# Moving the second half of each attention unit's transposes and products one slot earlier

## The chip, the cores and the metric

The kernel runs on one core of one Trainium2 chip. The metric is the device time in microseconds of one execution; three runs of the kernel before have a median of 1816.32 us.

## The reference

Linear attention over 8 batches, 8 heads, 576 tokens and a head width of 64, then two MLPs over the 4608 tokens:

```python
q_s = exp(q - max(q, -1)); q_s /= sum(q_s, -1) + 1e-9
k_s = exp(k - max(k, 2));  k_s /= sum(k_s, 2) + 1e-9
kv = einsum('bhsd,bhse->bhde', k_s, v)
x = einsum('bhsd,bhde->bhse', q_s, kv)            # to (4608, 512)
xn = x / sqrt(mean(x * x, -1) + 1e-6) * rms_g
y = (silu(xn @ w_gate) * (xn @ w_val)) @ w_out    # d_ff 1536
h = y @ w_in
out = (h * sigmoid(1.702 * h)) @ w2_out           # d_ff 2048
```

## The kernel before

All products are made of three passes over numbers split in a high and a low part (hi, lo). The first MLP runs over 9 tiles of 512 tokens (j = 0 to 8). A tile has 36 slots, three for each of its 12 chunks of the hidden width: slot 3n is the long product with w_gate (wg, 12 matmuls), slot 3n+1 the one with w_val (wv), slot 3n+2 the output product of the chunk before (into ps_acc, weights wo). The second MLP follows in a part of its own, which the change does not reach.

In the gaps between the long products of tile j stands the attention of batch j+1: four units (c = 0 to 3) of two heads each, for the tiles 0 to 6. The steps of a unit (unit_steps, from line 303 on) are:

- s0: maximum of k over the tokens of a partition (DVE, L316). s1: transpose of it (L323) and its maximum (L327); q less its maximum (L330, L331). s2: transpose back (L335) and k less the maximum (L336).
- s3: the exponentials of k and q (ACT, L354: ke, qe); loads of the next unit's k, q and v on SP; the sums of qe and their reciprocals (DVE, L360 to L362); qe divided by them (L363: on POOL for batches 0 and 1, so in tile 0, and on DVE from tile 1 on).
- s4: k times v, 20 small matmuls (L370); on DVE its normalisation into kvH and kvL, the high and low part (L378 to L385).
- qT(0), qT(1): transposes of the first and second half of qe (L399), copied to qH (ACT, L407) and qL (DVE, L408). The halves are 256 and 320 tokens wide; in even batches (odd tiles) the first half is the one of 256, two transposes, and in odd batches that of 320, a narrow transpose and two full ones.
- att(0), att(1): three matmuls with kvH and kvL for each half (L414 to L416), copied to xr (ACT, L422).

The order is written by hand. The table AT (L782) gives the slot of each of the nine steps, to which 6c is added for unit c; within a slot the long product and what belongs to it come first, then the steps in the order of units, then what else is put there. After the steps, `squares(c)` is put at the slot AT[-1] + 6c (L797): ACT squares the unit's xr (L439, L442), and for c > 0 DVE adds it (L444). Slots of the part 0 end with `split_out_weight` (from tile 1 on), which splits a weight into wo on ACT (L160) and POOL (L161). In tile 0 the weights are also decoded in every slot (L148 to L157). In slot 30 `total` sums the squares on PE (L449).

All PSUM banks of these steps come from one pool of two, in the order in which the steps are recorded:

```python
bufs = {"att": 2, "gv": 2, "acc": 4}[tag]
return ps.tile([P, 512], F32, tag=tag, bufs=bufs, name=f"ps_{tag}")
...
order = sorted((AT[s] + 6 * c, c, s) for c in range(len(mine)) for s in range(STEPS))
...
put(j, AT[-1] + 6 * c, squares, c)
```

Of the kernel before, what the change touches and what calls it, by code (L numbers as in the profile page):

```python
# [20 lines left out]
def attention_glu_mlp(  # L21
# [708 lines left out]
    with tc.manual_schedule():  # L730
# [48 lines left out]
        def put(j, slot, fn, *args):  # L779
            plan[j][slot].append(lambda: fn(*args))  # L780

        AT = (-1, 1, 2, 3, 4, 6, 7, 9, 10)  # L782

        for j in range(NTILE):
            mine = [(j + 1) * NC + c for c in range(NC) if (j + 1) * NC + c < len(units)]
            for c, u in enumerate(mine):
                steps[u] = unit_steps(u)
            order = sorted((AT[s] + 6 * c, c, s) for c in range(len(mine)) for s in range(STEPS))
            for slot, c, s in order:
# [4 lines left out]
            if j + 1 < NTILE:  # L794
                squares, total, spread, scale = norm_steps(j + 1)
                for c in range(NC):
                    put(j, AT[-1] + 6 * c, squares, c)  # L797
                put(j, 30, total)
# [275 lines left out]
```

## Time and profile before

| what | us |
|---|---|
| median of three runs (1816.26 to 1817.03) | 1816.32 |
| the profiled execution | 1816.74 |
| its span, first to last instruction | 1814.9 |
| PE busy, whole span | 1742.3 (96%) |
| DVE busy | 1203.9 (66%) |
| ACT busy | 779.9 (43%) |
| POOL busy | 396.1 (22%) |

The engines are PE (TensorE), DVE (VectorE), ACT (ScalarE), POOL (GpSimd) and SP, which here issues loads and stores. Times within the span are in microseconds from its start. Tile 0 lies from 59.1 to 212.6, tile 1 from 212.6 to 324.2, and so on by 111.6 us to tile 6; the last two tiles have no attention. A matmul's end in the profile is modelled, so rows of PE overlap a little.

### The profile page before, as it was taken

What the parts mean: (1) busy time and instruction counts of PE and PEld (TensorE: products, weight loads), DVE (VectorE), ACT (ScalarE), POOL (GpSimd) and SP (SyncE); (2) the same over time, 40 slices, a digit from 0 to 9 for tenths busy, and PEclk for the clock granted to TensorE, in tenths of its full rate; (3) what the DMA queues carried; (4) which work ended last, traced back from release to release, by engine and by line L of the source; (5) the groups of instructions that cost most, each with busy time, mean ns of one, the idle gap of its engine ahead of it and who ended that gap; (6) DMA issues with size and microseconds to landing.
All of it is one profiled execution on the core that took longest, in us unless ns stands there. A gap on an engine that the chain in (4) does not pass through costs nothing.

```text
span 1814.9 us, 26699 instructions
## 1 busy us (share of the span) xinstructions
PE 1742.3 (96%) x10092; PEld 1543.3 (85%) x10092; DVE 1203.9 (66%) x2017; ACT 779.9 (43%) x1304; POOL 396.1 (22%) x360
## 2 busy tenths in 40 slices
PE   5777999999999999999999999999999999999998
PEld 4565788888888888888888879999999899999998
DVE  7999875775757657575323347556546797777785
ACT  4555544444444444443312236444435543333332
POOL 4666512212121221211111434000002640000000
PEclk9898999999999999999999999999999999999999
DMA  5344341322323232220001015434444544444432
GB/s 156 124 134 127 101 123 55 106 84 67 103 65 105 75 95 75 60 75 20 24 1 47 24 58 186 140 113 141 140 148 159 197 129 139 129 128 128 128 117 82
DMA packets 202001, 186.31 MB, mean 103 GB/s; under 512 B 58256, under 2 KB 183696, under 8 KB 201872
## 3 DMA queue, kind: packets, MB, share of 16 engines
q1 hardware_dynamic: 191888, 166.51, 29.7%
q10 hardware_dynamic: 9984, 18.09, 2.7%
q8 instruction: 79, 1.29, 0.3%
q14 instruction: 50, 0.41, 0.1%
HBM read 119.54 MB, written 65.01 MB: 102 GB/s over the span
## 4 chain that ended last, share of the span: by engine, by line
PE 85%; DVE 10%; issue 2%; DMA 1%; ACT 1%; POOL 0%; SPq 0%; DVEq 0%; ACTq 0%; POOLq 0%
PE ps_gv L493 29%; PE ps_in L639 19%; PE ps_out L984 17%; PE ps_acc L493 15%; PE ps_att L370 1%; PE ps_att L399 1%; DVE uf L722 1%; DVE w L151 1%; DVE raw L151 1%; DVE raw L550 1%; DVE raw L154 1%; DVE u L509 1%; PE ps_att L449 1%; DVE y L998 0%; DVE m L316 0%
## 5 line engine op out<-in xcount | busy, mean ns | idle before, releaser
L984 PE MATMUL ps_out<-w2o,uf 128*128 128x256 f32 x3024 | 366.8, 284 | 5.4 <-DVE uf L722 4.7
L984 PEld LDWEIGHTS ps_out<-w2o,uf 128*128 128x128 f32 x3024 | 365.1, 193 | 7.1 <-DVE uf L722 5.6
L639 PE MATMUL ps_in<-xf,w2i 128*128 128x384 f32 x2016 | 349.9, 334 | 2.4 <-ACT ev L530 2.4
L639 PEld LDWEIGHTS ps_in<-xf,w2i 128*128 128x128 f32 x2016 | 349.4, 188 | 3.1 <-ACT ev L530 2.8
L493 PE MATMUL ps_acc<-u,wo 128*128 128x512 f32 x1296 | 328.6, 403 | 5.7 <-POOL wo L161 5.7
L493 PE MATMUL ps_gv<-xs,wg 128*128 128x512 f32 x1296 | 322.5, 397 | 7.1 <-POOL wg L161 5.6
L493 PE MATMUL ps_gv<-xs,wv 128*128 128x512 f32 x1296 | 319.2, 395 | 0.4 <-DVE s L834 0.4
L493 PEld LDWEIGHTS ps_gv<-xs,wg 128*128 128x128 f32 x1296 | 243.4, 191 | 62.4 <-POOL wg L161 7.7
L493 PEld LDWEIGHTS ps_acc<-u,wo 128*128 128x128 f32 x1296 | 244.9, 193 | 58.6 <-POOL wo L161 6.8
L493 PEld LDWEIGHTS ps_gv<-xs,wv 128*128 128x128 f32 x1296 | 240.6, 189 | 49.4 <-POOL wv L161 1.2
L161 POOL TENSOR_TENSOR wo<-raw,wo 128x512 fp32r<-128x512 f32 x108 | 142.3, 1318 | 495.5 <-ACT wo L160 477.5
L828 ACT ACTIVATE s<-ps_gv 128x512 f32<-128x512 f32 x108 | 64.5, 598 | 428.6 <-PE ps_gv L493 428.6
L834 DVE TENSOR_TENSOR s<-s,ps_gv 128x512 f32<-128x512 f32 x108 | 73.9, 684 | 198.3 <-PE ps_gv L493 174.3
L624 ACT ACTIVATE h<-h 128x384 f32<-128x384 f32 x144 | 74.4, 525 | 115.2 <-DVE h L661 85.1
L157 POOL TENSOR_TENSOR w<-w,stage 128x512 int32<-128x512 int32 x56 | 73.5, 1312 | 220.2 <-DVE w L154 70.9
L550 DVE TENSOR_TENSOR raw<-raw 128x256 f32<-128x256 f32 (+1 forms) x236 | 108.0, 500 | 11.8 <-DMA raw<-w2d 7.6
L661 DVE TENSOR_TENSOR h<-h,ps_in 128x384 f32<-128x384 f32 x144 | 78.0, 553 | 49.8 <-PE ps_in L639 49.3
L719 ACT ACTIVATE uf<-raw 128x1792 fp32r<-128x1792 f32 x36 | 61.2, 1701 | 86.0 <-PE ps_out L984 53.1
L554 POOL TENSOR_TENSOR w2o<-raw,w2o 128x256 fp32r<-128x256 f32 x35 | 28.2, 843 | 275.9 <-DMA u<-h 270.1
L722 DVE TENSOR_TENSOR uf<-raw,uf 128x1792 fp32r<-128x1792 f32 x36 | 74.4, 2067 | 18.7 <-ACT uf L719 18.7
L510 DVE TENSOR_TENSOR u<-s,u 128x512 fp32r<-128x512 f32 x108 | 82.8, 767 | 3.7
L360 DVE TENSOR_REDUCE qs<-qe 128x10 f32<-128x640 f32 x32 | 26.2, 820 | 85.7 <-ACT qe L354 85.6
(139 smaller groups left out, 1863.2 us busy)
## 6 DMA issues: line engine op xcount, KB each, us to landing
u<-h SPq DMA_DIRECT2D x192, 192.0 KB, 1.9
stage<-in_moe_w_out_dram SPq DMA_DIRECT2D x28, 512.0 KB, 3.6
raw<-u SPq DMA_DIRECT2D x24, 512.0 KB, 4.3
x<-ev ACTq DMA_DIRECT2D x36, 256.0 KB, 2.0
stage<-in_moe_w_in_dram SPq DMA_DIRECT2D x16, 512.0 KB, 3.7
w2d<-w SPq DMA_DIRECT2D x32, 256.0 KB, 3.3
v_sb<-in_v_dram SPq DMA_DIRECT2D x60, 128.0 KB, 3.2
out_dram<-y ACTq DMA_DIRECT2D x30, 256.0 KB, 4.3
```

Of the source, the lines that this page charges most:

```text
L157: return lambda: nc.gpsimd.tensor_tensor(dst, dst, lo, op=ALU.add)
L161: nc.gpsimd.tensor_tensor(dst[:, 1, :], src, f(dst[:, 0, :]), op=ALU.subtract)
L493: nc.tensor.matmul(t, w(a), x(e), start=first and i == 0, stop=last and i == 2)
L510: nc.vector.tensor_tensor(u[:, 1, :], s, f(u[:, 0, :]), op=ALU.subtract)
L550: engine.tensor_tensor(raw[:, o], raw[:, a], raw[:, b], op=op)
L624: nc.scalar.activation(dst, src, AF.Gelu_apprx_sigmoid)
L639: nc.tensor.matmul(t, w[:, a, s, c * P : (c + 1) * P], xfac[i, p, c][:, e, :], start=p in (1, 6, 5) and c == 0 and k == 0, stop=c == 1 and ...
L661: nc.vector.tensor_tensor(v, v, t, op=ALU.add)
L722: nc.vector.tensor_tensor(w[:, 1], raw, f(w[:, 0]), op=ALU.subtract)
L828: nc.scalar.activation(s, tg, AF.Silu)
L834: nc.vector.tensor_tensor(s, s, tv, op=ALU.mult)
L984: nc.tensor.matmul(t[:, i * Q : (i + 1) * Q], u[:, a, LEFT[p] - 1, i * P : (i + 1) * P], w[:, e, m % 2, :], start=m == 0 and i == 0 and n ...
```

## The change

Two entries of the table: the second transposes qT(1) go from slot 7 to slot 6, behind the first, and the second products att(1) from slot 10 to slot 9, behind the first. As `squares` takes its slot from the last entry, it moves a slot ahead as well.

```diff
-        AT = (-1, 1, 2, 3, 4, 6, 7, 9, 10)
+        AT = (-1, 1, 2, 3, 4, 6, 6, 9, 9)
```

On PE, around the transposes of the second unit of tile 1 (wg, wv are the long products, x12 is twelve matmuls in a row; the waits are on semaphores of the engine named), before:

```order
L493 MATMUL ps_gv<-xs,wg_977 128x512 x12
L399 MATMUL ps_att<-ident,qe 128x128 [waits DVE_49,PE_49,Activation_49]
L399 MATMUL ps_att<-ident,qe 128x128
L493 MATMUL ps_gv<-xs,wv_1033 128x512 [waits DVE_49]
L493 MATMUL ps_gv<-xs,wv_1033 128x512 x11
L399 MATMUL ps_att<-ident,qe 128x128 [waits DVE_49,PE_49]
L399 MATMUL ps_att<-ident,qe 128x128
L399 MATMUL ps_att<-ident,qe 128x64
L323 MATMUL ps_att<-ident,m_2212 128x128 [waits DVE_49]
```

and now:

```order
L493 MATMUL ps_gv<-xs,wg_986 128x512 x12
L399 MATMUL ps_att<-ident,qe 128x128 [waits DVE_49,PE_49,Activation_49]
L399 MATMUL ps_att<-ident,qe 128x128
L399 MATMUL ps_att<-ident,qe 128x128 [waits DVE_49,PE_49]
L399 MATMUL ps_att<-ident,qe 128x128
L399 MATMUL ps_att<-ident,qe 128x64
L493 MATMUL ps_gv<-xs,wv_1033 128x512 x12
L323 MATMUL ps_att<-ident,m_2212 128x128 [waits DVE_49]
```

The second half, with its wait on DVE, stands ahead of the wv product; s1 of the next unit stays behind it.

On ACT, from the copy of the second unit's first att half on, tile 1, before:

```order
L422 ACTIVATE xr<-ps_att 128x256
L354 ACT_TABLE_LOAD
L354 ACTIVATE ke<-k_sb 128x2x5x64
L354 ACTIVATE qe<-q_sb 128x2x5x64
L160 ACTIVATE wo<-raw_1088 128x512
L422 ACTIVATE xr<-ps_att 128x320
L442 ACTIVATE sqb<-xr 128x512
```

and now:

```order
L422 ACTIVATE xr<-ps_att 128x256
L422 ACTIVATE xr<-ps_att 128x320
L354 ACT_TABLE_LOAD
L354 ACTIVATE ke<-k_sb 128x2x5x64
L354 ACTIVATE qe<-q_sb 128x2x5x64
L442 ACTIVATE sqb<-xr 128x512
L160 ACTIVATE wo<-raw_1095 128x512
```

The second copy stands ahead of the next unit's exponentials, and the square ahead of the weight's copy.

On DVE, in the third unit of tile 1, from the division of qe to kvL, before:

```order
L363 TENSOR_TENSOR qe<-qe,qs 128x640
L834 TENSOR_TENSOR s<-s,ps_gv 128x512
L509 CAST u<-s 128x512
L510 TENSOR_TENSOR u<-s,u 128x512
L378 TENSOR_SCALAR rs<-ps_att 128x1
L379 RECIPROCAL rs<-rs 128x1
L382 TENSOR_SCALAR kvH_76<-ps_att,rs 64x64 x2
L385 SCALAR_TENSOR_TENSOR kvL_78<-ps_att,rs,kvH_76 64x64 x2
L444 TENSOR_TENSOR sqa<-sqa,sqb 128x512
```

and now:

```order
L363 TENSOR_TENSOR qe<-qe,qs 128x640
L444 TENSOR_TENSOR sqa<-sqa,sqb 128x512
L834 TENSOR_TENSOR s<-s,ps_gv 128x512
L509 CAST u<-s 128x512
L510 TENSOR_TENSOR u<-s,u 128x512
L378 TENSOR_SCALAR rs<-ps_att 128x1
L379 RECIPROCAL rs<-rs 128x1
L382 TENSOR_SCALAR kvH_76<-ps_att,rs 64x64 x2
L385 SCALAR_TENSOR_TENSOR kvL_78<-ps_att,rs,kvH_76 64x64 x2
```

The addition of the squares stands ahead of the steps that make kvL.

## Rows read from the trace of the kernel before

**Rows 1.** Windows, tiles 0 and 1: us; busy PE, PEld, DVE, ACT, POOL; clock, DMA, GB/s.

```profile
59.10:212.60 153.50, 121.82 (x540) 93.09 (x538) 148.48 (x194) 86.40 (x148) 97.93 (x72) 0.88 0.43 132
212.60:324.20 111.60, 111.58 (x577) 90.96 (x576) 73.98 (x135) 51.00 (x87) 24.45 (x19) 1.00 0.28 84
```

**Rows 2.** Timeline of DVE, tile 1: start, us, what, [idle before <- releaser].

```profile
246.20 0.82 DVE L360 TENSOR_REDUCE qs<-qe 128x10 f32<-128x640 f32 x1 [3.57 <-ACT qe L354]
247.05 1.03 DVE L361 TENSOR_SCALAR qs<-qs 128x10 f32<-128x10 f32 x1
248.36 0.83 DVE L363 TENSOR_TENSOR qe<-qe,qs 128x640 f32<-128x640 f32 x1
...
251.91 0.60 DVE L385 SCALAR_TENSOR_TENSOR kvL<-ps_att,rs,kvH 64x64 fp32r<-64x64 f32 x2
...
271.89 0.70 DVE L444 TENSOR_TENSOR sqa<-sqa,sqb 128x512 f32<-128x512 f32 x1
272.50 1.32 DVE L316 TENSOR_REDUCE m<-k_sb 128x128 f32<-128x640 f32 x1
```

**Rows 3.** Timeline of PE, tile 1, around the second unit's steps.

```profile
242.42 0.28 PE L414 MATMUL ps_att<-qH,kvH 128*128 128x256 f32 x1
...
246.02 0.95 PE L370 MATMUL ps_att<-v_sb,ke 128*64 128x65 f32 x20
...
252.48 0.38 PE L399 MATMUL ps_att<-ident,qe 128*128 128x128 f32 x2
...
255.45 0.58 PE L399 MATMUL ps_att<-ident,qe 128*128 128x128 f32 x3
```

**Rows 4.** Timelines: kvL and first transposes, tile 1 unit 0, tile 2 unit 1.

```profile
233.01 0.60 DVE L385 SCALAR_TENSOR_TENSOR kvL<-ps_att,rs,kvH 64x64 fp32r<-64x64 f32 x2
233.14 0.38 PE L399 MATMUL ps_att<-ident,qe 128*128 128x128 f32 x2
...
363.63 0.60 DVE L385 SCALAR_TENSOR_TENSOR kvL<-ps_att,rs,kvH 64x64 fp32r<-64x64 f32 x2
...
364.26 0.64 PE L399 MATMUL ps_att<-ident,qe 64*128 64x64 f32 x3
```

**Rows 5.** Timeline of ACT and POOL, tile 1, around the second unit's exponentials.

```profile
243.11 0.38 ACT L422 ACTIVATE xr<-ps_att 128x256 f32<-128x256 f32 x1
...
244.80 0.74 ACT L354 ACTIVATE ke<-k_sb 128x640 f32<-128x640 f32 x1
245.44 0.72 ACT L354 ACTIVATE qe<-q_sb 128x640 f32<-128x640 f32 x1
246.07 0.61 ACT L160 ACTIVATE wo<-raw 128x512 fp32r<-128x512 f32 x1
246.59 0.47 ACT L422 ACTIVATE xr<-ps_att 128x128 f32<-128x128 f32 x2
...
246.76 1.29 POOL L161 TENSOR_TENSOR wo<-raw,wo 128x512 fp32r<-128x512 f32 x1 [2.69 <-ACT wo L160]
246.96 0.63 ACT L439 ACTIVATE sqa<-xr 128x512 f32<-128x512 f32 x1
```

**Rows 6.** Timelines of POOL and DVE, tile 0: L361 free, L510 under POOL.

```profile
68.44 0.17 DVE L361 TENSOR_SCALAR qs<-qs 128x10 f32<-128x10 f32 x1
...
73.58 1.48 POOL L161 TENSOR_TENSOR wv<-w,wv 128x512 fp32r<-128x512 f32 x1
73.94 1.67 DVE L510 TENSOR_TENSOR u<-s,u 128x512 fp32r<-128x512 f32 x1
```

**Rows 7.** Waits of PE, whole span: us in total, times, longest us.

```profile
PE ps_att L449 <- DVE sqa L444: 4.0, 2, 2.0
```

**Rows 8.** Timelines of PE and DVE, tile 0.

```profile
92.33 0.31 PE L414 MATMUL ps_att<-qH,kvH 128*128 128x320 f32 x1
...
93.44 0.81 DVE L336 TENSOR_TENSOR k_sb<-k_sb,ps_att 128x640 f32<-128x640 f32 x1
...
101.98 2.56 PE L493 MATMUL ps_gv<-xs,wg 128*128 128x512 f32 x10 [1.63 <-POOL wg L161]
```

## The prediction

> **What bounds the kernel now.** I read the busy time by stretch first [rows 1]. In tile 0 (59.1 to 212.6 us) VectorE (DVE) is busy for 148.48 of 153.50 us and TensorE (PE) for 121.82: weight decoding on DVE sets the pace, and a wait of PE costs nothing while DVE goes on. In tile 1, as in tiles 2 to 6 that repeat it, PE is busy for 111.58 of 111.60 us: there every wait of PE is added to the time in full, and nothing that any other engine gains is worth anything. So the question is where PE would wait after the change, and for how long.
>
> Attention work is done four units to a tile. Each unit's small products (transposes L399, attention products L414 to L416) stand in gaps between the long products. All of them take their PSUM banks in turn from a pool of two (tag "att"). The sequence of a unit is s4, first qT, second qT, the next unit's s1 and s2, first att, second att, the next s4. So the second qT writes into the bank of s4, and the second att into the bank of s2. The change keeps this sequence and only closes up the times; the program's order, shown above, has the two halves next to each other on PE, so it does what it says.
>
> **Second qT: the new wait.** The bank of s4 is free when its last reader on DVE, the second half of kvL (L385), is done. In tile 1, unit 1, the kvL pair ends at 251.91 + 0.60 = 252.51 [rows 2], and the first qT starts at 252.48 [rows 3]. Now the second qT comes a whole product later, at 255.45 [rows 3], with 2.9 us to spare. After the change it is due right behind the first. Two transposes show 0.38 us and three 0.58 [rows 3]; in tiles 1, 3 and 5 the first half has two, and I take the second half as due 0.22 us after the first transpose. In tiles 2, 4 and 6 the first half is the three, one of them narrow, with 0.64 [rows 4]: due after 0.48.
>
> How late kvL stands to the first transpose today: +0.03 in tile 1, unit 1 (above), and I take units 2 and 3 alike, since their steps have the same order up to there. In unit 0 it is 233.01 + 0.60 - 233.14 = +0.47 [rows 4], in tile 2, unit 1, 363.63 + 0.60 - 364.26 = -0.03 [rows 4].
>
> **What makes kvL later (units 1 to 3 of a tile).** The next unit's exponentials share a slot with the attention products.
> - ACT. Today the copy xr of the first half ends at 243.11 + 0.38 = 243.49, and the exponentials follow; the second half's copy (0.47) comes behind them, at 246.59 [rows 5]. Now it goes first. The second half's products follow the first's directly on PE, and the copy of the first shows that three are out within 0.69 us (242.42 to 243.11 [rows 3, 5]), so ACT need not wait for them much beyond 243.49. Shift of the exponentials: 0.46. The second one, qe, ends at 246.16 + 0.46 = 246.62.
> - The square (0.63 [rows 5], about 0.55 to the next start) now stands ahead of the weight copy wo (L160). POOL's subtraction L161, today at 246.76, goes to 246.76 + 0.46 + 0.55 = 247.77 and ends at 249.06.
> - DVE. L360 starts 0.04 after qe, takes 0.82 and ends at 247.48. L361 takes 0.17 when it is free [rows 6] and is held to 248.08 today, 0.03 behind POOL's end at 248.05 [rows 2, 5]. Now it slips in ahead of POOL: 247.68. L362 ends at 247.93, and L363 comes to start at 247.96, in the middle of POOL's run. A two-input SBUF subtraction in that position is held: L510 began at 73.94 under a POOL run that ended at 75.06, and ended at 75.61, 0.55 behind it [rows 6]. L363 is 0.14 longer, so it ends 0.69 behind POOL, at 249.75, where today it ends at 249.19 [rows 2]. Everything to kvL moves by 0.55 (0.45 in the even tiles, whose second half is narrower).
> - L444 adds the squares for the second and third unit. It moves from behind kvL to ahead of it: 0.61 more, from its start to the next one's (271.89 to 272.50 [rows 2]), in units 2 and 3.
>
> The trace has no L363 under a POOL run. The Trainium skill, "SBUF — State Buffer", section "Who interferes with whom", says that a DVE instruction with two SBUF inputs contends with a GpSimd instruction that reads SBUF, and that the one that comes first blocks the other fully; by that L363 is held and the sum is the one below, and without it the sum is that of the first rival. The row of L510 agrees with the page.
>
> **The sum for tiles 1 to 6.** A wait is today's lateness, plus the shift, plus 0.05 from the end of one engine's work to the start of another's (qe's end to L360: 0.04 [rows 2, 5]), less the time at which the second half is due.
> - Odd tiles: unit 0, 0.47 + 0.05 - 0.22 = 0.30 (nothing shifts there, no attention products precede it); unit 1, 0.03 + 0.55 + 0.05 - 0.22 = 0.41; units 2 and 3, 0.61 more, 1.02 each. Together 2.75, three tiles: 8.25.
> - Even tiles: unit 0, which I take as late as in the odd ones at most, 0 to 0.04, taken as 0; unit 1, -0.03 + 0.45 + 0.05 - 0.48 is below 0; units 2 and 3, 0.60 each. Together 1.2, three tiles: 3.6.
>
> That makes **+11.9 us** in 15 waits. If the transposes were due 0.2 later it would be 3 less; if L361 were held as well (POOL 0.26 earlier than I have it), L363 would end about 0.1 later, or 1.5 in all.
>
> **What is hidden.** The second att takes the bank that the k subtraction (L336) reads; in the steady tiles that is done before: DVE has stood idle for 3.57 us when L360 starts at 246.20 [rows 2], so all that precedes it was done by 242.63, and the second att is due no earlier than 242.42 [rows 3] plus the first half's three products. The s4 products wait for ke: it ends today at 244.80 + 0.74 = 245.54 [rows 5] and will at 246.00, the products start at 246.02 [rows 3]; the cover is used up but just holds: 0, at most 0.2 on 18 units. DVE's multiplication for the long product and POOL's wo come up to 1.2 us later; their readers on PE come more than a product later. The loads that s3 issues on SP go out 0.46 later, and SP's order is unchanged. In unit 3 of each tile two gaps fall away altogether; the steady rows show no cost of a gap beyond its products, so 0, at most -1.
>
> **Tile 0.** Two things pull. The last L444 stands a slot earlier, and one of the two waits of 2.0 us for it at the tile's end (4.0 in two [rows 7]) should go; I take -2 and at most -4. Against it, the second att now waits for L336, which ends at 94.25, while the first att stands at 92.33 [rows 8]: the half is due near 92.7 and PE stands for 1.6 us, three times. PE has the time, but the exponentials behind the copy are late too, and DVE may starve: 0 to +4.8, taken as 0, since DVE decodes in between.
>
> Profiled execution: 1816.7 + 11.9 - 2 = 1826.6 us; the median of the runs lies 0.4 below that execution. **Forecast: 1826 us, slower by about 0.55%.** Bounds of this case: 1820 to 1833.
>
> **The rivals.**
> 1. L363 is not held by POOL (it slips ahead, or its broadcast input spares it). Then it ends at 247.96 + 0.83 = 248.79, 0.40 earlier than today, and pays for most of L444's 0.61. What is left is 0.30 for unit 0 and about 0.08 for units 2 and 3 in odd tiles: 1.4 us, against -2 in tile 0. Time 1816, **not slower**. It decides at a POOL start after 247.96, 0.2 later than I have it. For it: the margin is small; against it, L510. Chance 0.14.
> 2. The waits don't matter and tile 0 gives more: PE gains the 4.0 us of both waits for L444 and the closed gaps 1 us: 1812. For it: no row forbids it; against it, the explicit wait on DVE in the new order. Chance 0.05.
> 3. The short waits upset the clock. Fifteen waits, each followed by a product at the lower of the two clock levels, would each lose about what such a product takes at full clock, some 2.7 us (ten of its twelve matmuls take 2.56 [rows 8]): +40, 1867. Against it: in tile 0 PE waited 1.63 us and the ten matmuls behind it took 2.56 us [rows 8], the 0.25 each of full clock; no wait above is longer. The Trainium skill, "TensorE: Matmul & The Clock Gate", section "A second HAM failure mode: psum-queue depth-cycling", tells of a kernel in which short idling while PSUM banks were cycled made the clock swing; the row here does not show it. Chance 0.03.
>
> **How the numbers follow.** Forecast case 0.78, rivals 0.14, 0.05 and 0.03. About 0.2% (3.6 us) is what a measurement of this kernel tells from no change. Faster by more than that is rival 2: 0.05. Within it is rival 1 and the low edge of the forecast case: 0.18. Slower is the rest: 0.77. The range takes in rival 1 and the bounds of the forecast case: 1815.5 to 1833.
>
> **What would show it.** PE's waits in tiles 1 to 6, today without an entry, would list L399 on DVE kvL L385, some 15 times with about 1 us as the longest, and the windows of the odd tiles would be near 114.4 us long, of the even ones near 112.8, with PE's busy time unchanged. DVE's L363 would show about 1.8 us in units 1 to 3, and L361 0.17. If L363 stands at 0.83 the first rival holds. If PE waits at L414 for L336, or at L370 for ke, I have misjudged a cover; if tile 0 is longer than 153.5 us, DVE starved there.

## The result and the profile after

The changed kernel takes 1830.86 us (median of six runs, 1829.28 to 1831.61) where the kernel before takes 1816.67 (six runs, 1816.07 to 1818.12): a ratio of 1.0076, 95% interval 1.0066 to 1.0086. It is slower by 14.2 us. The forecast was 1826 in a range of 1815.5 to 1833. The sign held, and so did the mechanism for tiles 1 to 6; the sum had +9.9 us (11.9 less 2 in tile 0) where 14.2 were measured. Of the eleven executions of e7 below, one ran at a mean granted clock of 0.75 and took 2159 us; no ratio counts it.

The profiled execution spans 1829.2 us, 14.3 more than that of before. First, windows of the changed kernel: tiles 1 to 6 together, then tiles 2 to 4 one by one, each from the spread matmuls L464 of the tile before to its own (us; busy PE, PEld, DVE, ACT, POOL; clock, DMA, GB/s).

```profile
215.00:890.00 675.00, 665.96 (x3421) 537.08 (x3420) 429.48 (x785) 297.46 (x500) 133.81 (x104) 1.00 0.25 75
...
320.19:433.14 112.95, 112.14 (x578) 90.45 (x576) 73.57 (x135) 50.74 (x83) 23.39 (x18) 1.00 0.28 83
433.14:547.74 114.60, 112.57 (x577) 90.85 (x576) 73.45 (x135) 50.74 (x83) 23.40 (x18) 1.00 0.28 82
547.74:660.84 113.10, 112.17 (x578) 90.44 (x577) 73.57 (x135) 50.95 (x87) 23.37 (x18) 1.00 0.28 83
```

A tile was 111.60 us long, with PE busy for all but 0.02 of it [rows 1]. Now tile 3 takes 114.60 and tiles 2 and 4 take 112.95 and 113.10, and PE's busy time falls short of the length by 0.8 to 2.0: PE stands still, at a granted clock of 1.00, the upper of its two levels. Its waits, in the same stretch (us in total, times, longest):

```profile
PE ps_att L399 <- DVE kvL L385: 8.9, 18, 0.9
```

Before, this list was empty. The 8.9 us count from modelled ends of the matmuls; the weight loads (PEld) ahead of the same transposes show the gaps somewhat larger, and those of s4 wait for ke:

```profile
PEld ps_att L399 <- PE ps_att L399: 12.6, 18, 1.1
PEld ps_att L370 <- ACT ke L354: 9.0, 24, 0.4
```

Before, the first of these rows was not there, and the second read:

```profile
PEld ps_att L370 <- ACT ke L354: 2.7, 6, 0.4
```

One place at close quarters, the second unit of tile 1, to be laid beside [rows 2, 3, 5]. First ACT in the changed kernel (start, us, what):

```profile
245.04 0.80 ACT L422 ACTIVATE xr<-ps_att 128x256 f32<-128x256 f32 x3
245.86 1.28 ACT L354 ACT_TABLE_LOAD   x1
...
248.42 0.61 ACT L439 ACTIVATE sqa<-xr 128x512 f32<-128x512 f32 x1
248.94 0.61 ACT L160 ACTIVATE wo<-raw 128x512 fp32r<-128x512 f32 x1
```

Then POOL (at the end of the row the idle time before it and its releaser):

```profile
249.63 1.29 POOL L161 TENSOR_TENSOR wo<-raw,wo 128x512 fp32r<-128x512 f32 x1 [3.46 <-ACT wo L160]
```

Then DVE:

```profile
248.55 0.82 DVE L360 TENSOR_REDUCE qs<-qe 128x10 f32<-128x640 f32 x1 [3.82 <-ACT qe L354]
249.40 0.17 DVE L361 TENSOR_SCALAR qs<-qs 128x10 f32<-128x10 f32 x1
...
249.86 1.74 DVE L363 TENSOR_TENSOR qe<-qe,qs 128x640 f32<-128x640 f32 x1
...
254.32 0.60 DVE L385 SCALAR_TENSOR_TENSOR kvL<-ps_att,rs,kvH 64x64 fp32r<-64x64 f32 x2
```

And PE, there and in the third unit of tile 1:

```profile
254.44 0.38 PE L399 MATMUL ps_att<-ident,qe 128*128 128x128 f32 x2
255.07 0.61 PE L399 MATMUL ps_att<-ident,qe 128*128 128x128 f32 x3 [0.25 <-DVE kvL L385]
255.61 1.65 PE L493 MATMUL ps_gv<-xs,wv 128*128 128x512 f32 x6
...
274.30 0.38 PE L399 MATMUL ps_att<-ident,qe 128*128 128x128 f32 x2
275.54 0.61 PE L399 MATMUL ps_att<-ident,qe 128*128 128x128 f32 x3 [0.85 <-DVE kvL L385]
276.08 2.14 PE L493 MATMUL ps_gv<-xs,wv 128*128 128x512 f32 x8
```

Read in this order: all three copies of xr (x3) stand ahead of the exponentials; the square is done before the weight's copy, so POOL starts 0.23 us after L361 began; L361 slips through in 0.17 instead of 1.03; L363 falls under POOL's run (249.63 to 250.92) and ends at 251.60, 0.68 behind it; kvL ends at 254.92, 0.48 after the first transpose, and the second half starts 0.15 after that. In the third unit L444 stands in between as well, and the second half starts 1.24 us after the first instead of 0.63.

That the bank ties the second half to kvL is read from this trace. In all 18 waits it starts 0.14 to 0.15 us behind kvL's end, whether that end comes 0.4 or 1.1 us after the first transpose. It reads qe, which was ready 3.5 us earlier (251.60), and nothing that kvL writes; what it shares with kvL's step is the bank, by the order of the pool. The first half, which takes the other bank, starts ahead of kvL's end.

### The profile page after: what moved, and what is told of

It reads as the page before. It is cut to its first block, busy times and chain, and to the rows that moved or that the text cites. A ratio compares the mean times of both kernels' runs of the same rounds, so it can differ in the third digit from the quotient of the medians.

```text
span 1829.2 us, 26705 instructions
## 1 busy us (share of the span) xinstructions
PE 1747.3 (96%) x10092; PEld 1541.4 (84%) x10092; DVE 1203.3 (66%) x2017; ACT 779.4 (43%) x1304; POOL 395.7 (22%) x360
## 3 DMA queue, kind: packets, MB, share of 16 engines
q8 instruction: 79, 1.29, 0.3%
## 4 chain that ended last, share of the span: by engine, by line
PE 76%; DVE 14%; ACT 5%; issue 2%; SPq 1%; DMA 1%; POOL 0%; ACTq 0%; DVEq 0%; POOLq 0%
PE ps_gv L493 24%; PE ps_in L639 19%; PE ps_out L984 18%; PE ps_acc L493 12%; DVE qe L363 2%; ACT L354 2%; DVE u L510 1%; DVE qs L360 1%; DVE u L509 1%; DVE s L834 1%; PE ps_att L399 1%; ACT qe L354 1%; ACT ke L354 1%; DVE kvL L385 1%; DVE kvH L382 1%
## 5 line engine op out<-in xcount | busy, mean ns | idle before, releaser
L493 PE MATMUL ps_acc<-u,wo 128*128 128x512 f32 x1296 | 320.7, 396 | 4.3 <-POOL wo L161 4.3
L493 PE MATMUL ps_gv<-xs,wv 128*128 128x512 f32 x1296 | 324.3, 400 | 0.2 <-POOL wv L161 0.2
L493 PEld LDWEIGHTS ps_acc<-u,wo 128*128 128x128 f32 x1296 | 240.2, 189 | 57.9 <-POOL wo L161 5.6
L161 POOL TENSOR_TENSOR wo<-raw,wo 128x512 fp32r<-128x512 f32 x108 | 142.3, 1318 | 510.9 <-ACT wo L160 479.5
L360 DVE TENSOR_REDUCE qs<-qe 128x10 f32<-128x640 f32 x32 | 26.2, 820 | 94.2 <-ACT qe L354 94.1
L510 DVE TENSOR_TENSOR u<-s,u 128x512 fp32r<-128x512 f32 x108 | 83.2, 770 | 3.7
```

What stands on the lines that cost most here:

```text
L161: nc.gpsimd.tensor_tensor(dst[:, 1, :], src, f(dst[:, 0, :]), op=ALU.subtract)
L493: nc.tensor.matmul(t, w(a), x(e), start=first and i == 0, stop=last and i == 2)
L510: nc.vector.tensor_tensor(u[:, 1, :], s, f(u[:, 0, :]), op=ALU.subtract)
```

## The experiments

Each run's profile gives two stretches, read from the starts of three rows of PE: the first product wg of the program, s4 (L370) of the first unit in tile 1, and the spread matmuls (L464) of tile 6. These are the three in the changed kernel; before, they start at 45.68, 226.68 and 873.84.

```profile
45.95 0.79 PE L493 MATMUL ps_gv<-xs,wg 128*128 128x512 f32 x1 [1.50 <-ACT xs L484]
...
228.09 0.95 PE L370 MATMUL ps_att<-v_sb,ke 128*64 128x65 f32 x20
...
888.65 0.60 PE L464 MATMUL ps_att<-ident,rms 128*128 128x128 f32 x4
```

"Tile 0" is the first difference, "tiles 1 to 6" the second, each from one execution. What follows, to the end of the span, lies between 940.2 and 943.2 us in all of them; its work is the same but in e5. The ratio is against the kernel before in runs made along with it; e9 and e10 ran on another chip than e1 to e8.

| kernel | tile 0, us | tiles 1 to 6, us | ratio of the medians (95%) |
|---|---|---|---|
| before | 181.00 | 647.16 | 1 |
| the change | 182.14 (+1.1) | 660.56 (+13.4) | 1.0076 (1.0066 to 1.0086) |
| e1, transposes alone | 180.33 (-0.7) | 649.18 (+2.0) | 1.0005 (0.9996 to 1.0015) |
| e2, products alone | 182.36 (+1.4) | 647.69 (+0.5) | 1.0008 (0.9999 to 1.0017) |
| e3, squares a slot later | 181.83 (+0.8) | 652.78 (+5.6) | 1.0027 (1.0016 to 1.0038) |
| e4, change in tile 0 alone | 182.01 (+1.0) | 647.12 (0.0) | 1.0001 (0.9992 to 1.0011) |
| e5, POOL without L161 | 182.23 (+1.2) | 649.58 (+2.4) | one run, 1819.7 us |
| e6, unused bank tile | 180.42 (-0.6) | 647.17 (0.0) | one run, 1815.84 us |
| e7, exponentials early, halves together | 180.60 (-0.4) | 648.07 (+0.9) | 0.9999 (0.9989 to 1.0008) |
| e8, exponentials early, halves apart | 179.79 (-1.2) | 648.03 (+0.9) | 0.9999 (0.9990 to 1.0008) |
| e9, s4 in a bank of ps_gv | 180.61 (-0.4) | 670.85 (+23.7) | 1.0132 (1.0118 to 1.0146) |
| e10, transposes in tile 0 alone | 179.23 (-1.8) | 647.17 (0.0) | 0.9994 (0.9985 to 1.0003) |

**One half of the change at a time.** e1 moves the transposes alone and leaves products and squares:

```diff
-        AT = (-1, 1, 2, 3, 4, 6, 7, 9, 10)
+        AT = (-1, 1, 2, 3, 4, 6, 6, 9, 10)
```

> Only the second transposes are moved; att(1) and the squares stay. Bank theory (the loss is PE waiting in the second transposes for kvL, which the att half has made later): kvL keeps its time, so tiles 1 to 6 keep 0.3 us of wait in unit 0 of the odd tiles and next to none elsewhere, +1 us in all; in tile 0 the second qL fills time in which DVE is held by POOL anyway, -1.4. Total -0.5 (-2 to +1.5). Rival (standing together is what costs, five transposes in a row): most of the 13 us of tiles 1 to 6 stays.

e2 moves the products, and the squares with them:

```diff
-        AT = (-1, 1, 2, 3, 4, 6, 7, 9, 10)
+        AT = (-1, 1, 2, 3, 4, 6, 7, 9, 9)
```

> Only att(1) and with it the squares are moved; the second transposes stay behind the wv product. Bank theory: kvL comes 0.5 to 1.2 us later, but the second transposes have 2.9 us to spare, so tiles 1 to 6 lose nothing; tile 0 loses 2 to 3 us by DVE waiting for the exponentials (no gain there from qL). Total +2.5 (+1 to +4). Rival (the later exponentials cost by themselves, through the s4 products or a later kvL): tiles 1 to 6 keep about 13 us.

In tiles 1 to 6 the one costs 2.0 us and the other 0.5, together they cost 13.4: almost 11 us belong to neither alone. The transposes make the second half due early; the products make kvL late. With the products alone L363 takes 1513 ns in the mean, as in the change (1514, of 24), and no wait for kvL is listed; with the transposes alone three short ones are (0.7 us in all), in the first unit of the odd tiles, where kvL was late before the change. Both runs cost more in these tiles than was expected of them (+1 and nothing).

**The squares' slot.** e3 is the change with the squares put where they stood.

```diff
-                    put(j, AT[-1] + 6 * c, squares, c)
+                    put(j, AT[-1] + 1 + 6 * c, squares, c)
```

> Both halves moved as in the change, but the squares put back one slot later, where they stood before. Bank theory with the two delays priced apart: L444 is behind kvL again (0.61 less in units 2 and 3), and POOL's wo subtraction starts 0.55 earlier, so L361 instead of L363 is held and kvL is 0.46 late. Waits of 0.3 us in every unit of the odd tiles and about 0 in the even ones: tiles 1 to 6 lose 4 us instead of 13, tile 0 as in the change, +1.4. Total +5.5 (+4 to +7). Rival (the squares don't matter, the copy ahead of the exponentials does it all): total near +14.

Groups of DVE in 215 to 890 us (busy, mean ns, idle), of e3:

```profile
L361 DVE TENSOR_SCALAR qs<-qs 128x10 f32<-128x10 f32 x24 | 24.8, 1034 | 0.8
L363 DVE TENSOR_TENSOR qe<-qe,qs 128x640 f32<-128x640 f32 x24 | 19.8, 826 | 0.8
```

and of the change:

```profile
L363 DVE TENSOR_TENSOR qe<-qe,qs 128x640 f32<-128x640 f32 x24 | 36.3, 1514 | 0.8
L361 DVE TENSOR_SCALAR qs<-qs 128x10 f32<-128x10 f32 x24 | 9.4, 390 | 0.8
```

With the squares back, POOL holds L361 as before and spares L363, and the 13.4 us fall to 5.6. So 7.8 us come from the square's place (on ACT ahead of the weight's copy, on DVE ahead of kvL; the two are not taken apart), which the change moves only because `squares` takes its slot from the last entry of the table.

**POOL's run taken away.** e5 is the change with the low part of the weights set by a memset from tile 1 on, in place of the subtraction L161.

```diff
-        split_weight(w, f(weight["raw", n // 2][:, n % 2, :]))
+        raw = f(weight["raw", n // 2][:, n % 2, :])
+        if low:
+            split_weight(w, raw)
+        else:
+            nc.scalar.activation(w[:, 0, :], raw, AF.Copy)
+            nc.gpsimd.memset(f(w[:, 1, :]), 0.0)
```

(`low` is a new argument of this function, `def split_out_weight(n, low=True)`, and is false from tile 1 on.)

> The changed kernel, but from tile 1 on POOL's subtraction for the low part of w_out is replaced by a memset to zero (the low part of w_out is left out in tiles 1 to 8). A memset reads nothing from SBUF. Hold theory (L363 is late because POOL's subtraction holds it): L363 shows 0.83 us instead of 1.8, kvL comes about 1 us sooner, waits for kvL remain in unit 0 of the odd tiles (0.5) and 0 to 0.3 in units 2 and 3: tiles 1 to 6 lose 2 to 5 us against before instead of 13. Rival (the copy ahead of the exponentials makes all of the lateness, the hold none): about 13 as in the change.

Groups of DVE of e5, whose lines stand five further down (L368 is L363, L366 is L361):

```profile
L368 DVE TENSOR_TENSOR qe<-qe,qs 128x640 f32<-128x640 f32 x24 | 19.8, 826 | 0.8
L366 DVE TENSOR_SCALAR qs<-qs 128x10 f32<-128x10 f32 x24 | 4.2, 173 | 0.8
```

Both run free, L444 still stands ahead of kvL, and 2.4 us are left. So POOL's run has a part in most of the loss. What the new hold of L363 costs by itself e5 does not say, for it also takes away the hold of L361, which the kernel before had in all 24 units (1032 ns in the mean). That is why the 0.5 us of wait expected in the first unit of the odd tiles are not there: kvL now ends ahead of the first transposes. What is left are waits in the third and fourth unit, 0.4 us each in tile 1, and those of s4 for ke. The memset ran while neither L361 nor L363 did, so whether it would have held them was not seen.

Before, too, the end of L363 followed POOL's, by way of L361: 1.14 us behind it (249.19 against 248.05 [rows 2, 5]); now it is 0.68 behind, 0.46 less. But POOL's run, which began 5.72 us ahead of the first transposes (246.76 and 252.48 [rows 3, 5]), now begins 4.81 ahead (249.63 and 254.44), 0.91 later. The difference, 0.45, is what kvL lost: it ends 0.48 after the first transpose where it was 0.03.

**Tile 0 alone.** e4 has the new entries in tile 0 and the old ones elsewhere (the line stands in the loop over the tiles, in place of the one table).

```diff
+            AT = (-1, 1, 2, 3, 4, 6, 6, 9, 9) if j == 0 else (-1, 1, 2, 3, 4, 6, 7, 9, 10)
```

> The change in tile 0 alone, the old table from tile 1 on. If the stages add up: the 1.1 to 1.4 us by which tile 1 started later in the changed kernel, and nothing after: total +1.3 (0 to +2.5). Rival (tile 0 gives back 2 us, as the forecast had it, and the later start is something else's): -2.

In the profile tile 0 keeps its +1.0, and tiles 1 to 6 are as before to 0.04 us: what tile 0 loses does not grow behind it. In the medians, 1817.6 against 1817.3, it can't be told from no change.

**The bank.** e6 takes an unused tile from the pool ahead of the first transposes, in the kernel before, to turn the banks round:

```diff
+            if i == 0 and tag == "att":
+                bank(tag)
             t = bank(tag)
```

> The kernel before, all slots as they were; one bank of the pool of two is taken and left unused ahead of the first transposes, so that these take the bank of s4 (and the second ones the other). Bank theory: the first transposes now wait for kvL, 0.5 us in unit 0 of each tile, 0.1 or less in units 1 to 3: tiles 1 to 6 lose 3 to 5 us, listed as L399 on kvL L385, with no step moved. Rival (the banks have no part in it, moving the steps has): the same time as before and no such wait.

Nothing changed, in the waits of tiles 1 to 6 or in the time. Had the pairing been turned, this would speak against the theory; the likelier reading is that a tile which nobody writes takes no place in the order, so that it was not turned. No run shows that, and e6 decides nothing. e9 goes at it in another way, with the change as it is but s4 in the other pool:

```diff
         def s4():
-            t = bank(tag)
+            t = bank("gv" if tag == "att" else tag)
```

> The changed kernel, but in the tiles the small products of s4 take their bank from the pool of the long products (ps_gv, two banks) and not from ps_att. So the second transposes no longer share a bank with them, with the order of the steps left as it is. The price: the long product wg two slots behind s4 now gets the bank of the wv product before s4, whose last reader is DVE's L834. In the changed kernel's trace L834 ends in tile 1 at 232.30 and 252.21 where that wg starts at 231.82 and 251.71, so 0.6 us late with 0.14 for the release, and another 0.6 in units 2 and 3, where L444 stands ahead of it. Theory of the bank: no wait for kvL is left at L399 in tiles 1 to 6, and in its place stand some 24 waits of PE at L493 (ps_gv) for L834, 0.5 to 1.2 us each, about 3.3 us in a tile, 20 in all: tiles 1 to 6 +20 us against before, time about 1837 us. If the second transposes were late for another reason than the bank (DVE's order, qe, the copies), the waits at L399 stay, 19 in tiles 1 to 6, and the time is 1831 or more with both kinds listed.

PE's waits of e9 from 212 to 890 us, all of them:

```profile
PE ps_gv L493 <- DVE s L834: 15.5, 24, 1.0
```

Timeline of PE of e9, second and third unit of tile 1, with kvL of the second:

```profile
250.15 3.06 PE L493 MATMUL ps_gv<-xs,wg 128*128 128x512 f32 x12 [0.39 <-DVE s L834]
252.21 0.60 DVE L385 SCALAR_TENSOR_TENSOR kvL<-ps_gv,rs,kvH 64x64 fp32r<-64x64 f32 x2
253.05 0.80 PE L399 MATMUL ps_att<-ident,qe 128*128 128x128 f32 x5
253.78 3.02 PE L493 MATMUL ps_gv<-xs,wv 128*128 128x512 f32 x12
...
270.88 3.02 PE L493 MATMUL ps_gv<-xs,wg 128*128 128x512 f32 x12 [0.98 <-DVE s L834]
```

The wait that the other pool's turn foretells stands there 24 times: that pool does hand out its two banks in the order of the steps. The price was 23.7 us where 20 were expected. The wait for kvL is gone in all 24 units, but that proves less than it seems to: the new wait holds PE back, so that kvL ends ahead of even the first transpose (252.81 and 253.05 here; by 0.19 to 0.32 in the 24 units), and a shared bank would have shown no wait either. No run here takes the bank away and leaves the times as they are; the bank rests on the reading given with the trace of the change. The second unit's rows also show the five transposes without a wait: 0.73 us from the first to the wv product.

**kvL earlier.** e7 moves the exponentials ahead of the attention products from tile 1 on, so that kvL comes early, and keeps both halves together; e8 is the same with the halves apart.

```diff
+            AT = (-1, 1, 2, 3, 4, 6, 6, 9, 10) if j == 0 else (-1, 1, 2, 2, 4, 6, 6, 9, 9)
```

```diff
+            AT = (-1, 1, 2, 3, 4, 6, 6, 9, 10) if j == 0 else (-1, 1, 2, 2, 4, 6, 7, 9, 10)
```

> From tile 1 on the halves stand together as in the change, but the exponentials (s3) go one slot earlier, ahead of the attention copies on ACT and of L834 on DVE; in tile 0 only the second transposes are moved. Bank theory: with qe 3 us earlier, kvL is set by the long product alone and is done long before the second transposes, so no wait for kvL is left in tiles 1 to 6, and the wait of s4 for ke in unit 0 (0.25 each) goes too: tiles 1 to 6 take 1 to 2 us less than before, tile 0 0.7 less. Total -2 (-3 to 0). Rival (standing together costs PE time by itself): tiles 1 to 6 stay several us above before.

> As the run with early exponentials, but with the halves apart in their old slots from tile 1 on. If standing together saves nothing by itself, tiles 1 to 6 take the same here as in that run, within 0.5 us: -1 to -2 against before. If the closed gaps save PE time, this one is slower than that run by 1 us or more.

No wait of PE's matmuls is listed in either, but neither is faster than before: +0.9 us in tiles 1 to 6 in both. The weight loads of s4 now wait for a copy; e7, from 215 to 890 us:

```profile
PEld ps_att L370 <- ACT xr L422: 6.1, 16, 0.4
```

The forecast of -1 to -2 us failed for both. Together or apart is the same to 0.04 us, so a gap that falls away gives nothing to be seen in these tiles; in e8 the weight loads' wait for the copy is shorter (3.9 us), and a gain of the closed gaps in e7 could be hidden by that.

**A last candidate.** e10 moves the transposes in tile 0 alone.

```diff
+            AT = (-1, 1, 2, 3, 4, 6, 6, 9, 10) if j == 0 else (-1, 1, 2, 3, 4, 6, 7, 9, 10)
```

> The kernel before with only the second transposes moved, and only in tile 0; attention products and squares as before. In the run with the transposes moved in all tiles, tile 0 became 0.7 us shorter and tiles 1 to 6 2.0 us longer; here the first should stay and the second go: tile 0 -0.7, tiles 1 to 6 within 0.1 of before, 1816 us, the one version that could stand below both kernels, though 0.7 us (0.04%) is under what five rounds can tell from none. If the -0.7 came from scatter between executions, tile 0 is within 0.2 of before.

It is the shortest profile of tile 0, but e1, e7, e8 and e10 have the same order there and lie between 179.23 and 180.60, with the kernel before and e6 at 181.00 and 180.42. The mean of the four, 179.99, is 0.7 below that of the two; the change, e4 and e5, with its order in tile 0, lie at 182.01 to 182.23. The four scatter by 1.4 us, so the 0.7 is not shown. In the medians, 1816.04 against 1817.1, it can't be told from no change. No version tried beats the kernel before by more than the measurement can tell.

## Why the prediction was right, and where it was off

**The second qT: right.** It waits for kvL, 0.15 us behind its end each time, and the bank of s4 is the one thing that ties the two; that costs full time, since PE had no idle time to give there (111.58 of 111.60 us busy in tile 1 [rows 1]).

**What makes kvL later: right, step by step.** L361 slips ahead (0.17) and L363 is held, 1.74 us for 0.83, ending 0.68 behind POOL where 0.69 was worked out from L510. By the Trainium skill ("SBUF — State Buffer", "Who interferes with whom") a DVE instruction with two SBUF inputs contends with a POOL instruction that reads SBUF; the 1.74 under the subtraction and the 826 ns of e5 without it agree. L444 adds its 0.6 in units 2 and 3. kvL ends 0.48 after the first transpose in the second unit, where the sum had 0.58.

**The sum for tiles 1 to 6: 13.4 for 11.9.** Take the time from the first transpose to the wv product, less that without a wait (0.73 in e9). Tile 1: 255.61 - 254.44 - 0.73 = 0.44 in the second unit and 276.08 - 274.30 - 0.73 = 1.05 in the third; the forecast said 0.41 and 1.02. The first unit shows 0.43 for 0.30. What was mis-sized is the term "0.05 from the end of one engine's work to the start of another's", taken from ACT to DVE: from kvL's end to the transposes it is 0.15. In units 1 to 3 the shift of kvL came out 0.1 smaller than forecast, and the two errors cancelled, which is luck; in the first unit nothing shifted, and the error shows. Read in this way (0.61 without a wait in the even tiles), all 24 units make 12.8 us. The wait of s4 for ke, "at most 0.2 on 18 units" and taken as 0, goes with the rest: e2 costs 0.5 without any wait for kvL, with 9.0 us of waits of the weight loads at L370 for ke, as in the change. "15 waits" was a slip of counting: the sum's own lines, four in an odd tile and two in an even one, make 18, and 18 are listed.

**Tile 0: the sign was wrong.** This term is the larger part of the miss: +1.1 us for the -2. The prediction took "one of the two waits of 2.0 us for it at the tile's end" as 2 us to be gained. Only one of the two lies there; the other, at 40.62, is ahead of tile 0. The one at the tile's end went, and PE waited for something else in its place, two slots later (timeline of PE, the changed kernel):

```profile
199.99 3.64 PE L493 MATMUL ps_acc<-u,wo 128*128 128x512 f32 x9 [1.96 <-POOL wo L161]
```

In e3, with the squares put back, the wait for L444 stands as before (1.9 us), and its tile 0 is no longer than the change's. The prediction's first paragraph had said that in tile 0 a wait of PE costs nothing while DVE goes on; then the -2 also gains nothing, and the term should have been 0. In the same way the second transposes wait for kvL in tile 0 too, the changed kernel first, then e10:

```profile
PE ps_att L399 <- DVE kvL L385: 10.5, 4, 2.8
...
PE ps_att L399 <- DVE kvL L385: 9.5, 4, 2.4
```

and e10 is no longer than before. The wait of the second att for L336, forecast at 1.6 us three times, is there once (1.4 us).

What DVE waits for is another matter. Its waits from 55 to 215 us in the changed kernel:

```profile
DVE qs L360 <- ACT qe L354: 4.4, 4, 1.9
```

Before, it is 1.0 us in one wait, and DVE's busy time from 59.1 to 212.6 us falls from 148.48 [rows 1] to 145.12. The second copy ahead of the exponentials makes qe late, and DVE stands. That is the starving that the prediction named (0 to +4.8) and set at 0. The five profiles that have 3.3 us or more of these waits (the change, e2 to e5) show 181.83 to 182.36 in tile 0; the seven that have 0 to 2.3 show 179.23 to 181.00, e9, with its products moved, among them. No run takes these waits alone away, so that they are the cause of the +1.1 is argued, not shown.

**The rivals.** The first (L363 not held) fell with 1514 ns in the mean of 24; the margin it hung on, POOL's start ahead of L363's, was 0.2 in the forecast and came out at 0.23 (249.63 and 249.86). The second (tile 0 gives more) fell with tile 0 longer. The third (the clock) fell: 18 waits and a granted clock of 1.00 from 215 to 890 us. The Trainium skill ("TensorE: Matmul & The Clock Gate", "A second HAM failure mode: psum-queue depth-cycling") tells of a clock that swings with short idling; these 18 waits did not make it do so.

## What to carry to other kernels

Before two steps are put next to each other on an engine, go through the order of their buffers: with a pool of two, the second one takes the place of the one before the first, and the slot between them was the time in which that was emptied. Look also at what moves along without being named (here the square, by an index from the end of the table): it made more than half of the loss. And in a stage that another engine paces, a wait of this one that falls away need not gain anything: count the waits of the engine that sets the pace.

## What the runs showed of the hardware

From the end of kvL on DVE to the start of the transposes that wait for it lie 0.15 us (254.92 to 255.07), against 0.04 from the end of ACT's qe to DVE's L360 [rows 2, 5]. POOL's run of 1.29 us, begun 0.2 to 0.3 us ahead of the DVE instruction that it met, cost that instruction about 0.9 whether it was short or long: 1.03 us for 0.17 on L361 before [rows 2, 6], 1.74 for 0.83 on L363 now.
